# Two head pairs a step, another layout for turned q, and a new order in a sparse-attention and maxout kernel

## The chip, the cores and the metric

One core of one Trainium2 chip. The metric is the device time of one execution in microseconds; times are medians over several runs. Engines in the profile: PE (TensorE matmul) and PEld (its weight loads), DVE (VectorE), ACT (ScalarE), POOL (GpSimd), SP (SyncE, which issues most DMAs here).

## What is computed

Four batches of eight heads, 768 positions, 64 numbers a head. Each query sees the keys less than 16 positions away, and 24 summaries of blocks of 32 positions (the maximum of k, the mean of v, with log 32 added to the score). The result, as 3072 tokens of 512 numbers, goes through a maxout layer. Cut to what matters:

```python
k_sum = k.reshape(B, H, nb, 32, D).max(axis=3)
v_sum = v.reshape(B, H, nb, 32, D).mean(axis=3)
scores_l = where(|i - j| < 16, q @ k.T / sqrt(D), -1e9)
scores_s = q @ k_sum.T / sqrt(D) + log(32)
a = softmax(concat([scores_l, scores_s], axis=-1))
x = (a @ concat([v, v_sum])).transpose(0, 2, 1, 3).reshape(B * S, H * D)
out = maximum(x @ w1, x @ w2) @ w_out
```

## The kernel before, in words

**Work units.** A head pair `hp` is two heads; each batch `b` has four. Each pair's queries fall in three groups `grp` of 256 positions. "Pair 20" means batch 2, pair 0.

**Preparation** (`prep`). k and q are loaded (`load_kq`, L392), cast to bf16 into `kqb`, and turned, so that the 128 numbers of the two heads lie on partitions. For the pairs in `CFG["turn"]` (20 to 23 and 30 to 33, so all of batches 2 and 3) both are turned by a DMA transpose on SP's queue (L519, into `kt`), for the others by PE (L515): k as three f32 transposes of bf16 pairs, q as six bf16 ones. Then `copy` (L483, a helper that records nearly every copy and cast, on whichever engine is chosen) places k in `kx` and q in `qx`. `kx` also takes the wrapped and shared parts and the block maxima `ks` (L541). `qx` holds each head on its own half of the partitions, with zeros in the other half.

**Scores** (`scores`, L599): four matmuls for a group, each 128 keys by 2 x 64 queries, into one PSUM bank. For the pairs in `turn`, q was loaded two tokens a partition, so `qx` has even and odd tokens apart, and the matmul writes every second word:

```python
rhs = qx[b, hp].ap[:].rearrange("p a (m j t) -> p a m j t", m=3, j=2)[:, :, m, :, at:at + half]
to = o[:, :, n0:n1].rearrange("p a (q j) -> p a j q", j=2)
```

In batch 0 the band mask is added on PE (L577, two matmuls with `hide`); in the other batches it is multiplied in on DVE after the exponential (L618, `mask`). The exponential is ACT's (L609), from the bank into `pb`.

**Values** (`values`, L645, L649): eight matmuls (sixteen in batch 0) of `pb` with `vx`, which holds v and the block means; a column of ones gives the sum of the weights. DVE takes its reciprocal (L659, `inv`) and multiplies (L661, into `xs`). Each two pairs are turned to `xt`: in batch 0 by PE (L677), later by a DMA transpose (L668).

**v** (`cast_v`, `spread_v`): v is loaded in pieces of 64 numbers (L401), cast to `vx`, and copied to shifted positions in `vx` ("odd", "all sums": copies of up to 64 x 3168 in batches 1 to 3). Block means are matmuls with `amean` (L451).

**Maxout** (`maxout`, `out_part`): max(a, b) = a + relu(b - a), so the hidden step uses `wd = w2 - w1` (L750, eight matmuls for each of four blocks, then a relu on ACT L759 or DVE L761). `w1o` = w1 x w_out, made once (L734). The output is `xt` x `w1o` (L777, four matmuls) plus `g` x `wo` (L784, eight), copied to `o` and stored.

**The order.** Each step is an `op` of a `Plan` with an estimated time, buffers it reads and writes, and a priority. `CFG["prios"]` gives the priorities and `CFG["engines"]` the engine of each step. `Plan.run` goes through a modelled time, gives every engine the ready step of least priority number, assigns buffer slots from `Ring`s (eight PSUM banks with limits for each kind: `kq` 2, `sc` 2, `av` 2, `mm` 3), and so fixes one instruction order for each engine. On the chip, engines run these fixed lists and wait on semaphores. In the model, DVE and POOL steps on their common port exclude each other.

**Start.** Set-up on POOL builds `hide` (L351 to L364) and `amean` (L370, L373). PE runs 32 matmuls on the identity (`warm_up`, L817) before its first work.

Of the kernel before, what the change touches and what calls it, by code (L numbers as in the profile page):

```python
# [26 lines left out]
    woc=600, wdp=30, lk="ADDP", lq="AAPA", lod="DPS", lse="DDD", lsr="DDS", lvc="DPPPDDAPPAPA", ltl="DDPD", ld=500,  # L27
    turn="20 21 22 23 30 31 32 33", lx="SSS",
)
CFG["prios"] = list(map(int, """  # L30
# [30 lines left out]
""".split()))  # L61
CFG["engines"] = "".join("""
TTPDDDPDAPDDDDDDDPPPDDDPAAPDPPSSSDADATAASSSPPPPTDDSSSPPPPTAASSSPDDPTADSSPPTDSSPPTDSSPATASSDDTDSASDSASDDTATDDADDADTAT
ATAATATDDDDPDATATATAPTATDDPDDDDTATATAATATDDPPPAATATATATDDTDDTATDDTDDTATDDTDDTATDDTDDTATDDTDDTDTDDTDDTDSSSDSSSASSSDSS
SDPDPATDADDTATDDAPADATADTADTADTDDTDDTDDPTATADDPDDATADTADTADTDDSTDDSTDDSPTATADPPAADTADTADTADTDDTDDTDDPTDTADDADAATADTA
DTADTDDSTDDSTDDSSSSPSSSPSSSASSSPPPASTAAPDSDSDDAAPPATADTADTADTDDTDDTDDPSPSDDAPAPATADTADTADTDDSTDDSTDDSDSASDDAADADTADT
ADTADTDDTDDTDDASASDDPPDDATADTADTADTDDSTDDSTDDSSSSPSSSASSSPSSSPPDSATADDPSDSADPPADDTADTADTADTDDTDDTDDDSDSADDADDDTADTAD
TADTDDSTDDSTDDSDSPSDDAPAAPTADTADTADTDDTDDTDDPSASDDAAPDATADTADTADTDDSTDDSTDDSTTATTATTATTATDTDTATDTTTDSTTTASTDTATATATT
TDSTTTDSTDTATATDTTTDSTTTASTATATATATTTDSTTTDSTATATATDTTTASTTTDSTDTATATATTTASTTTASTATATDTATTTDSTTTASTATDTATATTTASTTTAS
TATATATDTTTASTTTASTDTDTATATTTASTTTASTDTDTDTDTTTDSTTTASTATATDTDTTTDSTTTDSTTTAATTTDS  # L70
# [44 lines left out]
class Plan:  # L115
# [3 lines left out]
    BEGIN = {"PE": 1700, "ACT": 1300, "DVE": 850, "POOL": 500, "SP": 0}  # L119
    ISSUE, FIRST, DEPTH = 500, 1100, 5  # L120
# [4 lines left out]
    def op(self, on, us, fn, read=(), write=(), change=(), touch=(), prio=0.0, label="", port=False, issue=None):  # L125

        t = Task()
# [6 lines left out]
        t.fn, t.label, t.may_hold = fn, label, port  # L134
# [23 lines left out]
    def run(self):  # L158
        after = {t: [] for t in self.tasks}
        left = {t: len(t.deps) for t in self.tasks}  # L160
        can = dict.fromkeys(self.tasks, 0)
# [10 lines left out]
        order, events = [], [0, *busy.values()]  # L172
        heapify(events)
        while len(order) < len(self.tasks):
# [4 lines left out]
            for e, queue in open_.items():  # L179
# [7 lines left out]
                if e == "SP":  # L187
                    busy[e] = now + t.issue
                    end = max(sent[-1], now + self.FIRST) + t.us
                    sent.append(end)  # L190
                    t.done = end + max(0, min(1800, 900 + (end - 2300) * 3 // 40 * 10, (16800 - end) * 3 // 200 * 10))
                    heappush(events, busy[e])
                    heappush(events, end)
                else:
                    busy[e] = t.done = now + t.us
                    if t.port:
                        self.held[e] = t.done
# [14 lines left out]
def kernel(  # L212
# [25 lines left out]
    plan = Plan(CFG.get("prios"), CFG.get("engines"))  # L238
    op = plan.op
# [8 lines left out]
    banks = Ring(list(range(8)), {"kq": 2, "sc": 2, "av": 2, "mm": 3})  # L248
# [16 lines left out]
    pbr = Ring(tiles("pb", 10, [128, 4, 192], BF16))  # L265
# [32 lines left out]
    def fixed_parts():  # L298
# [20 lines left out]
        for i, t in enumerate(pbr.slots):  # L319
            once("D", pbr, i, {"D": 0.18, "P": 0.3}, lambda e, t=t: on(e).memset(t[:, :, 64:128], 0.0), i / 3 - 1)  # L320
# [25 lines left out]
        for hs in (slice(0, 4), slice(4, 8)):  # L346
            op("A", {"P": 0.9, "D": 0.85, "A": 1.5}, lambda e, hs=hs: zero(e, by_parity(0)[32:64, 1, :, hs]),
               write=[vx[0], apart_in], prio=0.15, label="gap")
# [5 lines left out]
        def make_hide():  # L354

            nc.gpsimd.memset(hide[:], 0.0)
            by = hide[:].rearrange("p (i w) q -> p w i q", w=2)
            for w, lo, hi, base in ((0, 0, 96, -16), (1, 64, 128, -16), (1, 0, 32, 48)):
                keep(by[lo:hi, w], base + window - 1, 1, [[0, 2], [-1, 64]])
                keep(by[lo:hi, w], window - 1 - base, -1, [[0, 2], [1, 64]])  # L360
            keep(by[96:128, 0], nb - 1, -1, [[0, 2], [0, 64]])
            keep(by[32:64, 1], nb - 1, -1, [[0, 2], [0, 64]])
            nc.gpsimd.memset(hide[64:128, 3, 48:64], NEG)
            nc.gpsimd.memset(hide[0:32, 3, 0:48], NEG)  # L364

        def make_amean():

            for at in (32, 96):
                am = amean[:, :, at:at + nb]
                nc.gpsimd.memset(am, 1.0)  # L370
                for base, mult, pat in ((0, 1, [[128, NM], [-block, nb]]),
                                        (block - 1, -1, [[-128, NM], [block, nb]])):
# [260 lines left out]
    def values(b, hp, grp, pb, prio, xt_on="D"):  # L633
# [20 lines left out]
        if hp % 2 == 0:  # L654
            xs[b, grp] = Buf(xsr)
# [233 lines left out]
```

## Time and profile before

| | us |
|---|---|
| median of 3 runs (range) | 184.57 (184.41 to 184.81) |
| the profiled execution | 183.87 |
| its span in the profile | 182.1 |
| busy: PE / DVE / ACT / POOL | 165.4 / 127.3 / 110.8 / 58.3 |
| instructions: PE / DVE / ACT / POOL | 1658 / 284 / 175 / 89 |

The span is what the profiler saw of the execution; 1.77 us of the execution's time lie outside it. The page gives busy time and 40 slices of the span (each digit is a busy share in tenths). The table of stages gives busy time in chosen stretches. The chain of waits follows the work that ended last back from the end. A matmul's recorded time holds its pipeline latency, so PE's cost of a group is read from the chain, where each piece is the time until the next one: eight hidden matmuls 0.87 us, four of 512 columns 0.86, eight value matmuls 0.24.

### The profile page before, as it was taken

Reading aid. Unit: us, or ns where it says so; the run is one execution under the profiler, and the core shown is the slowest. Engines: PE = TensorE matmul, PEld = TensorE weight load, DVE = VectorE, ACT = ScalarE, POOL = GpSimd, SP = SyncE. Lnnn points to the kernel's source line nnn. Section 1 sums busy time; section 2 is a strip of 40 time slices with the busy share of each in tenths; the row PEclk is TensorE's granted clock in tenths of the full one; section 3 lists DMA queues with packets and bytes.
Section 4 is the critical chain, followed back from the end, with each engine's and each line's share of the span. In section 5 each row is a group of like instructions: output and inputs, shape, how many; then the busy total and the mean of one; then the engine's idle time right before and its main releaser. Section 6 shows DMA issues by size and latency. Waiting matters only on the chain.

```text
span 182.1 us, 4281 instructions
## 1 busy us (share of the span) xinstructions
PE 165.4 (91%) x1658; PEld 119.2 (65%) x1658; DVE 127.3 (70%) x284; ACT 110.8 (61%) x175; POOL 58.3 (32%) x89
## 2 busy tenths in 40 slices
PE   6447998999999995998879999999999999999993
PEld 6335998996664542666557776585757777678453
DVE  6799986769495997999564876684776667334121
ACT  7669895883767779796567566244888453322010
POOL 7867859804050656723510122042121000000000
PEclk9957999999999999999999999999999999999999
DMA  5999999999999964269999799799998035241024
GB/s 180 341 258 271 349 351 363 365 353 219 306 245 218 272 214 124 84 162 229 228 236 238 192 232 283 163 227 239 214 193 229 0 61 144 38 122 48 0 81 155
DMA packets 69589, 37.45 MB, mean 206 GB/s; under 512 B 48640, under 2 KB 65600, under 8 KB 69568
## 3 DMA queue, kind: packets, MB, share of 16 engines
q1 hardware_dynamic: 69424, 37.11, 82.7%
q8 instruction: 13, 0.21, 0.6%
q10 hardware_dynamic: 144, 0.07, 0.1%
q14 instruction: 8, 0.07, 0.1%
HBM read 25.17 MB, written 6.29 MB: 173 GB/s over the span
## 4 chain that ended last, share of the span: by engine, by line
PE 57%; DVE 18%; DMA 12%; ACT 6%; issue 3%; SPq 1%; POOL 1%; POOLq 0%; ACTq 0%; DVEq 0%
PE banks L784 16%; PE banks L750 15%; PE banks L777 8%; PE banks L599 6%; DMA land<-in_v_dram 6%; PE banks L645 5%; DVE pb L618 4%; DMA xt<-xs 3%; DMA land<-in_k_dram 3%; ACT vx L483 3%; DVE kx L483 2%; DVE vx L483 2%; DVE ks L541 2%; PE banks L649 2%; PE banks L515 2%
## 5 line engine op out<-in xcount | busy, mean ns | idle before, releaser
L750 PE MATMUL banks<-xt,wd 128*128 128x256 bf16 x384 | 46.8, 273 | 1.1 <-DMA xt<-xs 1.1
L784 PE MATMUL banks<-wo,g 128*128 128x512 bf16 (+2 forms) x208 | 47.2, 362 | 0.0
L750 PEld LDWEIGHTS <-wd 128*128 128x128 bf16 x384 | 36.7, 98 | 8.2 <-issue 1.2
L609 ACT ACTIVATE pb<-banks 128x512 bf16<-128x512 f32 x48 | 27.0, 595 | 15.1 <-PE banks L599 14.3
L759 ACT ACTIVATE g<-banks 128x512 bf16<-128x512 f32 x29 | 17.2, 597 | 19.2 <-PE banks L750 19.0
L784 PEld LDWEIGHTS <-g 128*128 128x128 bf16 x208 | 18.6, 99 | 15.8
L777 PE MATMUL banks<-w1o,xt 128*128 128x512 bf16 (+2 forms) x104 | 24.7, 363 | 0.0
L645 PEld LDWEIGHTS <-pb 128*128 128x128 bf16 (+1 forms) x384 | 19.2, 98 | 7.5 <-DVE pb L618 3.0
L618 DVE TENSOR_TENSOR pb<-pb,mask 128x512 bf16<-128x512 bf16 (+1 forms) x48 | 21.1, 465 | 4.2 <-ACT pb L609 3.9
L599 PE MATMUL banks<-qx,kx 128*128 128x128 bf16 (+2 forms) x224 | 22.4, 254 | 1.7 <-POOL kx L483 1.5
L645 PE MATMUL banks<-vx,pb 128*128 128x65 bf16 (+1 forms) x384 | 21.1, 193 | 2.2 <-DVE pb L618 1.7
L599 PEld LDWEIGHTS <-kx 128*128 128x128 bf16 x224 | 18.9, 113 | 6.0 <-POOL kx L483 1.7
L761 DVE TENSOR_SCALAR g<-banks 128x512 bf16<-128x512 f32 x19 | 13.1, 691 | 11.8 <-PE banks L750 9.7
L661 DVE TENSOR_TENSOR xs<-banks,inv 128x256 bf16<-128x256 f32 x48 | 19.2, 418 | 0.5
L483 ACT COPY o<-banks 128x512 f32<-128x512 f32 (+1 forms) x14 | 7.9, 565 | 17.1 <-PE banks L784 16.0
L541 DVE TENSOR_REDUCE ks<-kx 128x24 bf16<-128x768 bf16 x16 | 15.1, 945 | 3.3 <-ACT kx L483 3.2
L659 DVE RECIPROCAL inv<-banks 128x4 f32<-128x4 f32 x48 | 7.9, 175 | 12.2 <-PE banks L645 9.5
L483 POOL CAST kqb<-land 128x768 bf16<-128x768 f32 x9 | 9.0, 1010 | 17.8 <-ACT o L483 8.6
L777 PEld LDWEIGHTS <-xt 128*128 128x128 bf16 x104 | 9.6, 100 | 7.3
L483 POOL COPY kx<-kx 128x384 bf16<-128x384 bf16 (+1 forms) x13 | 6.9, 532 | 22.8 <-ACT kx L483 14.0
L483 DVE COPY o<-banks 128x512 f32<-128x512 f32 (+2 forms) x12 | 7.5, 632 | 8.2 <-PE banks L784 8.1
L483 ACT CAST kqb<-land 128x768 bf16<-128x768 f32 x13 | 11.2, 866 | 2.0 <-DMA land<-in_q_dram 1.8
(88 smaller groups left out, 221.1 us busy)
## 6 DMA issues: line engine op xcount, KB each, us to landing
land<-in_k_dram SPq DMA_DIRECT2D x16, 384.0 KB, 5.7
land<-in_q_dram SPq DMA_DIRECT2D x16, 384.0 KB, 5.7
land<-in_v_dram SPq DMA_DIRECT2D x16, 384.0 KB, 6.8
out_dram<-o SPq DMA_DIRECT2D x19, 256.0 KB, 2.5
land<-in_moe_w_dram SPq DMA_DIRECT2D x8, 512.0 KB, 8.6
land<-in_moe_w_out_dram SPq DMA_DIRECT2D x4, 512.0 KB, 9.5
out_dram<-o SPq DMA_DIRECT2D x4, 224.0 KB, 2.7
xt<-xs SPq DMA_TRANSPOSE x18, 3.2
```

The costliest lines, as they stand in the source:

```text
L483: {"D": nc.vector.tensor_copy, "A": nc.scalar.copy, "P": nc.gpsimd.tensor_copy}[e](out=o, in_=i)
L541: op("D", 0.95, lambda e: nc.vector.tensor_reduce(out=ks.ap[:, 0:nb], in_=free(kt(), 128, [256, NM], [192, 2], [32, 2], [1, 32]), axis=AX. ...
L599: nc.tensor.matmul(out=to, lhsT=w, rhs=rhs, start=(mask_on != "T"), stop=(mask_on != "T" or (i == 3 and n1 == 64)))
L609: op("A", 0.61, lambda e: nc.scalar.activation(out=pv(), in_=bank(ps).rearrange("p (i w q) -> p i w q", w=2, q=64), func=ACT.Exp, scale=sc ...
L618: eng.tensor_tensor(out=o, in0=o, in1=m.to_broadcast([128, o.shape[1], 2, 64]), op=ALU.mult)
L645: nc.tensor.matmul(out=av()[:, u, a, :], lhsT=p[r], rhs=vx[b].ap[r, 4 * grp + 2 * u + par, h, 0:D + 1], start=(par == 0), stop=(b > 0 and ...
L661: op("D", 0.42, lambda e: nc.vector.tensor_tensor(out=x.ap[:, hp % 2], in0=av()[:, :, :, 0:D], in1=inv.ap[:].to_broadcast([128, 2, 2, D]), ...
L750: nc.tensor.matmul(out=bank(ps)[:, 256 * s:256 * s + 256], lhsT=wd[n].ap[:, c, 128 * s:128 * s + 128], rhs=x.ap[:, c, :], start=(c == 0), ...
L759: nc.scalar.activation(out=o, in_=bank(ps), func=ACT.Relu)
L761: nc.vector.tensor_scalar_max(out=o, in0=bank(ps), scalar1=0.0)
L777: nc.tensor.matmul(out=bank(ps, c1 - c0), lhsT=x.ap[:, c, sl], rhs=w1o[c].ap[:, cols], start=(c == 0), stop=False)
L784: nc.tensor.matmul(out=bank(ps, c1 - c0), lhsT=g.ap[:, f, sl], rhs=wo[f // 2].ap[:, f % 2, cols], start=False, stop=(f == FC - 1))
```

## The change

- **Two pairs at once.** `scores` now only fills a bank. A new function `weigh` takes the banks of two pairs of one group, with one exponential of 1024 elements into a `pb` of double size, and one mask product (for group 2 four smaller ones). `values` fills two banks, and takes one reciprocal and one product for both. An access pattern steps from one bank to the other. Limits of banks: `sc` 4, `av` 3. `attention` prepares two pairs, then goes through the groups.
- **Turned q.** The pairs in `turn` are now 22, 23, 30 to 33. Their q is loaded with token r of each 128 on partition r, in pieces of 64 numbers, so that `qx` is in plain order after the DMA transpose, and all scores take the plain form.
- **q turned in pairs.** Where PE turns q, it does so as for k: three f32 transposes of bf16 pairs. The cast puts the pairs side by side, and the place reads with a step of two.
- **Set-up.** `hide` is built for 64 columns and copied; `amean` is set with four memsets in place of six instructions on POOL.
- **v copies.** The large "odd" and "all sums" copies of batches 1 to 3 are cut in two halves of the blocks.
- **Order.** New `prios` and `engines`. The plan's model counts PE steps double before 12.5 us and has other start times. No warm-up matmuls (`warm=()`).

The diff, cut to its core:

```diff
-    turn="20 21 22 23 30 31 32 33", lx="SSS",
+    ... relu=1, warm=(), cold=12500,
+    turn="22 23 30 31 32 33", lx="SSS",
...
-    banks = Ring(list(range(8)), {"kq": 2, "sc": 2, "av": 2, "mm": 3})
+    banks = Ring(list(range(8)), {"kq": 2, "sc": 4, "av": 3, "mm": 2 + CFG["relu"]})
-    pbr = Ring(tiles("pb", 10, [128, 4, 192], BF16))
+    pbr = Ring(tiles("pb", 5, [128, 2, 4, 192], BF16))
...
+            nc.gpsimd.memset(hide[:, 0], 0.0)
+            keep(hide[0:96, 0], -16 + window - 1, 1, [[-1, 64]])
+            keep(hide[0:96, 0], window - 1 + 16, -1, [[1, 64]])
+            keep(hide[96:128, 0], nb - 1, -1, [[0, 64]])
...
-                       in_=src[b, 2 * hp:2 * hp + 2].rearrange("h (m p j) d -> p (h m) (j d)", m=3, j=2))
+                       in_=src[b, 2 * hp:2 * hp + 2].rearrange("h (m r) d -> r (h m) d", r=128))
...
+        parts = ((0, NM // 2), (NM // 2, NM)) if whole else ((0, NM),)
...
-                a, to, one = src.ap[:], bank(ps, S, BF16), identity
-                if n == 0:
-                    a, to, one = a.bitcast(F32), bank(ps), ident32
-                for j in range(J if n else J // 2):
+                for j in range(J // 2):
+                    nc.tensor.transpose(out=bank(ps)[:, 128 * j:128 * j + 128],
+                                        in_=src.ap[:].bitcast(F32)[:, 128 * j:128 * j + 128], identity=ident32[:])
...
-                    qx[b, hp].ap[r, a, :], order(qps, [1, 128], [128, J])[r]),
+                    qx[b, hp].ap[r, a, :], order(qps, [2, 128], [256, 3], [1, 2])[r]),
...
-                    if by_dma:
-                        m, at, half = c // 256, c % 256 // 2, (n1 - n0) // 2
...
+                    nc.tensor.matmul(out=view()[:, i // 2, :, i % 2, n0:n1], lhsT=w,
+                                     rhs=qx[b, hp].ap[:, :, c:c + n1 - n0], start=(mask_on != "T"),
...
+    def weigh(b, hp, grp, pss, prio, mask_on):
+        pb, tag = Buf(pbr), f"{b}{hp}{grp}"
+        op("A", {"A": 1.06}, lambda e: nc.scalar.activation(
+            out=spread(pb.ap[:, :, :, 0:128], [4 * 192, 2], [192, 4], [128, 2], [1, 64]),
+            in_=spread(bank_tile[:, pss[0].ap, 0:1], [512 * (pss[1].ap - pss[0].ap), 2], [128, 4], [64, 2], [1, 64]),
+            func=ACT.Exp, scale=scale),
+           read=pss, write=[pb], prio=prio, label=f"exp {tag}")
...
+            if grp < NG - 1:
+                both(spread(pb.ap[:, :, :, 0:128], [192, 8], [128, 2], [1, 64]), 0)
+            else:
+                for i in range(2):
+                    for n in range(2):
+                        both(spread(pb.ap[:, n:n + 1, 2 * i:2 * i + 2, 0:128], [192, 2], [128, 2], [1, 64]), i)
...
+        op("D", 0.19, lambda e: nc.vector.reciprocal(
+            out=inv.ap[:], in_=spread(bank_tile[:, pss[0].ap, D:D + 1], [step(), 2], [D + 1, 4])),
+           read=pss, write=[inv], prio=prio, label=f"inv {tag}")
+        op("D", 0.7, lambda e: nc.vector.tensor_tensor(
+            out=x.ap[:].rearrange("p n u a d -> p n (u a) d"),
+            in0=spread(bank_tile[:, pss[0].ap, 0:1], [step(), 2], [D + 1, 4], [1, D]),
+            in1=spread(inv.ap[:, 0:1, 0:1], [4, 2], [1, 4], [0, D]), op=ALU.mult),
+           read=[*pss, inv], write=[x], prio=prio, label=f"x {tag}")
...
-    for i in range(2):
-        warm_up(i)
     fixed_parts()
+    for n, us, release in CFG["warm"]:
+        warm_up(n, us, release)
```

More of the change, by code (lines that the diff above doesn't have):

```diff
@@ L118, with op @@
     LAG = {"PE": 250, "ACT": 200, "DVE": 150, "POOL": 200, "SP": 800}
-    BEGIN = {"PE": 1700, "ACT": 1300, "DVE": 850, "POOL": 500, "SP": 0}
-    ISSUE, FIRST, DEPTH = 500, 1100, 5
+    BEGIN = {"PE": 1700, "ACT": 2100, "DVE": 1660, "POOL": 310, "SP": 0}
+    ISSUE, FIRST, DEPTH, COLD = 500, 1100, 5, 12500
     def __init__(self, prios=None, engines=None):
         self.tasks, self.prios, self.engines = [], prios, engines
-    def op(self, on, us, fn, read=(), write=(), change=(), touch=(), prio=0.0, label="", port=False, issue=None):
+    def op(self, on, us, fn, read=(), write=(), change=(), touch=(), prio=0.0, label="", port=False, issue=None, release=0):
         t = Task()
@@ L160, in run @@
         left = {t: len(t.deps) for t in self.tasks}
-        can = dict.fromkeys(self.tasks, 0)
+        can = {t: t.release for t in self.tasks}
         for t in self.tasks:
@@ L171, in run @@
         sent = [0] * self.DEPTH
-        order, events = [], [0, *busy.values()]
+        order, events = [], [0, *busy.values(), *can.values()]
         heapify(events)
@@ L194, in run @@
                 else:
-                    busy[e] = t.done = now + t.us
+                    busy[e] = t.done = now + t.us * (2 if e == "PE" and now < self.COLD else 1)
                     if t.port:
@@ L354, in make_hide @@
         def make_hide():
[L356 to L372, printed above, removed]
-                    nc.gpsimd.affine_select(out=am, in_=am, compare_op=ALU.is_ge, fill=0.0, base=base,
-                                            channel_multiplier=mult, pattern=pat)
@@ new lines, in hide_odd, with hide_last, hide_wrap, ones_amean @@
+        def hide_odd(e, lo):
+            on(e).tensor_copy(out=hide[64 - lo:128 - lo, 1], in_=hide[lo:lo + 64, 0])
+        def hide_last(e):
+            on(e).tensor_copy(out=hide[:, 2:4], in_=hide[:, 0:2])
+        def hide_wrap(e):
+            on(e).memset(hide[64:128, 3, 48:64], NEG)
+            on(e).memset(hide[0:32, 3, 0:48], NEG)
+        def ones_amean(e):
+            for j in range(4):
+                on(e).memset(spread(amean[32 * j:32 * j + 32, 0, 32 + j:33 + j], [132, NM], [64, 2]), 1.0)
@@ new lines, in fixed_parts @@
+        half = [Buf(Ring([None])) for _ in range(4)]
+        op("P", 1.0, lambda e: make_hide(), write=[half[0]], prio=-9, label="hide")
+        for n in range(2):
+            op("D", {"D": 0.08, "P": 0.13}, lambda e, n=n: hide_odd(e, 64 * n), read=[half[0]], write=[half[1 + n]],
+               prio=-8, port=True, label="hide odd")
+        op("D", {"D": 0.08, "P": 0.18}, lambda e: hide_last(e), read=half[:3], write=[half[3]], prio=-8, port=True,
+           label="hide last")
+        op("D", {"D": 0.13, "P": 0.2}, lambda e: hide_wrap(e), read=half[3:], write=[hide_in], prio=-8, label="hide wrap")
@@ L379, in fixed_parts @@
+        op("D", {"D": 0.4, "P": 0.7}, lambda e: on(e).memset(amean[:], 0.0), write=[amean_in], prio=-2, label="amean")
+        op("D", {"D": 0.28, "P": 0.45}, lambda e: ones_amean(e), change=[amean_in], prio=0.2, label="amean")
         op("P", 0.4, lambda e: nc.gpsimd.tensor_scalar(
@@ L464, in spread_v, with aps @@
              read=[ps, blocks_in], write=[st], prio=prio, port=False, label=f"sums {tag}")
-        for w, r in ((0, s_rows), (1, slice(32, 64))):
-            def aps(w=w, r=r):
-                ds = slice(0, VW if whole or w == 0 else VW)
-                return (by_parity(b)[r, w, :, hs, ds],
-                        st.ap[r, hs, ds].rearrange("p h d -> p (h d)").rearrange(
-                            "p (o h d) -> p o h d", o=1, d=VW).to_broadcast([32, NM, n, VW]))
-            copy(engines[2], {"D": 0.12 + 6 * n * VW * 0.00028, "P": 0.06 + 6 * n * VW * 0.001,
-                              "A": 0.2 + 6 * n * VW * 0.00083, **({"S": 1.0} if whole else {})}, aps,
-                 read=[st, *([took] if w == 0 else [])], write=out, prio=prio, label=f"all sums {tag}{w}")
+        for i, (w, r, ms) in enumerate((w, r, m) for w, r in ((0, s_rows), (1, slice(32, 64))) for m in parts):
+            cols = (ms[1] - ms[0]) * n * VW
+            def aps(w=w, r=r, ms=ms):
+                return (by_parity(b)[r, w, slice(*ms), hs, :],
+                        st.ap[r, hs, :].rearrange("p h d -> p (h d)").rearrange(
+                            "p (o h d) -> p o h d", o=1, d=VW).to_broadcast([32, ms[1] - ms[0], n, VW]))
+            copy(engines[2], {"D": 0.07 + cols * 0.00029, "P": 0.1 + cols * 0.00086,
+                              "A": 0.2 + cols * 0.00083, "S": 0.5}, aps,
+                 read=[st, *([took] if w == 0 else [])], write=out, prio=prio, label=f"all sums {tag}{i}")
     def copy(engine, us, aps, label, port=True, **kw):
@@ L633, in values, with av, mm @@
     def values(b, hp, grp, pb, prio, xt_on="D"):
-        ps, tag = Buf(banks, "av"), f"{b}{hp}{grp}"
-        def av():
-            return bank(ps)[:, 0:4 * (D + 1)].rearrange("p (u a d) -> p u a d", u=2, a=2)
-        def mm():
+        pss, tag = [Buf(banks, "av") for _ in range(2)], f"{b}{hp}{grp}"
+        def av(n):
+            return bank(pss[n])[:, 0:4 * (D + 1)].rearrange("p (u a d) -> p u a d", u=2, a=2)
+        def mm(n):
             for u in range(2):
@@ L648, in mm @@
                         if b == 0:
-                            nc.tensor.matmul(out=av()[:, u, a, :], lhsT=p, rhs=apart[par][:, h, 0:D + 1],
+                            nc.tensor.matmul(out=av(n)[:, u, a, :], lhsT=p, rhs=apart[par][:, h, 0:D + 1],
                                              start=False, stop=(par == 1))
-        op("T", 0.24 if b else 0.47, lambda e: mm(), read=[pb, ready[b, hp], *([] if b else [apart_of[hp]])], touch=[vx[b]], write=[ps], prio=prio, label=f"values {tag}")
+        for n in range(2):
+            op("T", 0.26 if b else 0.49, lambda e, n=n: mm(n), read=[pb, ready[b, hp + n], *([] if b else [apart_of[hp + n]])],
+               touch=[vx[b]], write=[pss[n]], prio=prio, label=f"values {tag}{n}")
@@ L653, in values @@
         inv = Buf(invr)
-        if hp % 2 == 0:
-            xs[b, grp] = Buf(xsr)
+        x = Buf(xsr)
         if hp == 0:
             xt[b, grp] = Buf(xtr)
-        x, x_t = xs[b, grp], xt[b, grp]
-        op("D", 0.18, lambda e: nc.vector.reciprocal(out=inv.ap[:], in_=av()[:, :, :, D:D + 1]),
-           read=[ps], write=[inv], prio=prio, label=f"inv {tag}")
-        op("D", 0.42, lambda e: nc.vector.tensor_tensor(
-            out=x.ap[:, hp % 2], in0=av()[:, :, :, 0:D],
-            in1=inv.ap[:].to_broadcast([128, 2, 2, D]), op=ALU.mult),
-           read=[ps, inv], write=[x], prio=prio, label=f"x {tag}")
@@ L681, in values @@
         op("T", 0.23, lambda e: turn(), read=[x], write=[xp], prio=prio, label=f"turn x{tag}")
-        copy(xt_on, {"D": 0.42, "A": 0.62}, lambda: (
-            x_t.ap[:, hp - 1:hp + 1, :].rearrange("p h n -> p (h n)"), bank(xp, 512, BF16)), read=[xp], write=[x_t], prio=prio, port=False, label=f"xt {tag}")
-    invr = Ring(tiles("inv", 3, [128, 2, 2, 1], F32))
+        copy(xt_on, {"D": 0.43, "A": 0.6}, lambda: (
+            x_t.ap[:, hp:hp + 2, :].rearrange("p h n -> p (h n)"), bank(xp, 512, BF16)), read=[xp], write=[x_t], prio=prio, port=False, label=f"xt {tag}")
+    invr = Ring(tiles("inv", 3, [128, 2, 4], F32))
     w1t_part = [Buf(Ring([None])) for _ in range(4)]
@@ L743, in maxout, with hid, relu @@
         x, g = xt[b, grp], Buf(gr)
[L744 to L757 removed]
+        per = CFG["relu"]
+        for n0 in range(0, 4, per):
+            pss = [Buf(banks, "mm") for _ in range(per)]
+            for n in range(n0, n0 + per):
+                def hid(n=n, ps=pss[n - n0]):
+                    for s in range(2):
+                        for c in range(KC):
+                            nc.tensor.matmul(out=bank(ps)[:, 256 * s:256 * s + 256],
+                                             lhsT=wd[n].ap[:, c, 128 * s:128 * s + 128],
+                                             rhs=x.ap[:, c, :], start=(c == 0), stop=(c == KC - 1))
+                op("T", 0.87, lambda e, hid=hid: hid(), read=[x, wd[n]], write=[pss[n - n0]], prio=prio, label=f"hidden {b}{grp}{n}")
+            def relu(e, n0=n0, pss=pss):
+                o = spread(g.ap[:, 2 * n0:2 * n0 + 1, 0:1], [512, per], [1, 512])
+                i = spread(bank_tile[:, pss[0].ap, 0:1], [512 * (pss[-1].ap - pss[0].ap) or 512, per], [1, 512])
                 if e == "A":
[L759 removed]
+                    nc.scalar.activation(out=o, in_=i, func=ACT.Relu)
                 else:
[L761 to L763 removed]
+                    nc.vector.tensor_scalar_max(out=o, in0=i, scalar1=0.0)
+            op("A", {"A": 0.17 + 0.43 * per, "D": 0.13 + 0.56 * per}, relu, read=pss, write=[g], prio=-1, label=f"relu {b}{grp}{n0}")
         last = b == B - 1 and grp == NG - 1
```

133 lines of the change are left out of this document (48 added, 85 removed), and 58 rows, old and new, of the table turn.

## The prediction

> **What bounds the kernel now.** I read the page's slices first, then the table of stages, the chain of waits, the groups by form and the timeline where a row was in doubt.
>
> ```profile
> PE   6447998999999995998879999999999999999993
> ...
> PEclk9957999999999999999999999999999999999999
> ```
>
> TensorE has three lives: thin up to about 18 us, full to 50, with gaps to about 93, and then full to 179. The clock falls to half in the third slice although 32 warm-up matmuls ran at the start.
>
> ```profile
> 50.00:60.00 10.00, 9.80 (x72) 5.73 (x71) 7.79 (x13) 7.25 (x12) 2.51 (x3) 1.00 1.25 235
> ...
> 70.00:80.00 10.00, 8.15 (x104) 4.81 (x102) 9.70 (x21) 9.01 (x9) 7.23 (x4) 1.00 0.48 133
> ...
> 110.00:120.00 10.00, 10.00 (x95) 6.27 (x94) 7.64 (x20) 4.95 (x9) 1.09 (x3) 1.00 0.92 239
> ```
>
> Columns: stretch, length, busy time (instructions) of PE, PEld, DVE, ACT, POOL, clock, DMA share, GB/s. Summing what PE lacks: 8.2 us idle in 0 to 20 (its warm-ups count as busy), 0.7 in 20 to 50, 5.0 in 50 to 100, 0.8 at the tail. In 70 to 80 DVE is the full engine; from 100 on PE alone sets the time. So PE work taken from batches 2 and 3 is worth its full length, and work taken from DVE or ACT only before 93 us.
>
> ```profile
> 17.73 0.51 PE banks L515 x6
> ...
> 20.33 0.23 PE banks L599 x5
> ...
> 70.30 2.71 DVE pb L618
> ...
> 99.13 0.44 PE banks L599 x5
> ```
>
> This is the chain: start, length, what. The same five score matmuls of one group take 0.23 us in batch 0 and 0.44 in batch 2, both at clock 1.00. They differ in where they write: heads turned by DMA hold q as even and odd tokens apart, so each matmul writes PSUM in steps of two words. The mask of 2.71 us stands beside a GpSimd copy of 2.83 us (from 69.91); alone it takes 0.41.
>
> **The change part by part.** *q a token a partition, 64 numbers a piece.* Scores of turned heads take the plain form. Batches 2 and 3 have 2 x 4 pairs x 3 groups = 24 groups at 0.44 us, plain ones take 0.22 (four matmuls, chain at 18.45): 24 x 0.22 = 5.3 us less. All lie on PE, and from 92.6 to 160 us the chain itself holds 21 of them (9.24 us). Pairs 20 and 21 leave the turned list, so their k and q cost PE four turns of three f32 transposes, 0.34 us each (chain at 20.90): +1.4. Net on PE **-3.9 us**. SP loses four transposes with 1.2 to 1.3 us of issue each; the 0.35 us DVE places of those q become 0.56 us ones.
>
> The six loads that change are now in 256-byte pieces, as v's are:
>
> ```profile
> 8.00:9.00 1.00, 0.65 (x9) 0.43 (x7) 0.94 (x2) 0.45 (x3) 0.86 (x4) 1.00 1.07 372
> ...
> 10.00:11.00 1.00, 0.45 (x5) 0.18 (x2) 0.97 (x2) 0.00 (x0) 0.81 (x2) 0.50 1.35 229
> ```
>
> The first of these microseconds moves k and q in 1.5 KB pieces, the other v: 372 against 229 GB/s, and 216 in the next one. A load of 393 KB then takes 1.82 instead of 1.06 us at worst, 0.76 more. After 90 us v lands in 5.2 us (median) and q, in 512-byte pieces, in 5.8, so I take 0: PE is full there and works on other groups. Without that cover it costs 6 x 0.76 = 4.6 us. The Trainium skill ("DMA: Bandwidth & Descriptors", Specifications) asks for at least 512 bytes a piece for line rate; the v rows agree, and by it the 4.6 would be paid (a rival below).
>
> *q turned in pairs.* Three f32 transposes take PE as long as six bf16 ones (0.34 each way at full clock), so nothing there. The place on DVE changes form:
>
> ```profile
> L483 DVE COPY qx<-banks 64x768 bf16<-64x768 bf16 x7 | 6.7, 953 | 2.3 <-PE banks L515 2.2
> ...
> L483 DVE COPY kx<-banks 128x768 bf16<-128x768 bf16 x5 | 2.8, 555 | 1.2 <-PE banks L515 1.2
> ```
>
> q should take k's 555 ns: 0.40 less each. Against it the cast of q on ACT or POOL takes k's 1.05 us instead of 0.83, on engines at 61% and 32%: nothing on the path.
>
> *Two head pairs at once.* 48 exps, 48 reciprocals and 48 products become 24 of double size, and the masks of groups 0 and 1 become 12 (group 2 keeps four 256-element ones for two pairs).
>
> ```profile
> 79.26 0.24 DVE L659 RECIPROCAL inv<-banks 128x4 f32<-128x4 f32 x2
> 79.47 0.76 DVE L661 TENSOR_TENSOR xs<-banks,inv 128x256 bf16<-128x256 f32 x2
> ...
> 80.08 1.09 ACT L609 ACTIVATE pb<-banks 128x512 bf16<-128x512 f32 x2
> ```
>
> Two back to back already overlap: two reciprocals 0.24 (one alone 0.175), two products 0.76 (one 0.418), two exps 1.09 (one 0.595). A double product is about 0.69 (512 f32 from PSUM, the relu's row), a double exp about 1.02 (ACT's 1024-element place, 1.014). So a merged pair saves 0.06 to 0.16 on the reciprocal, 0.07 to 0.15 on the product, 0.07 to 0.17 on the exp, about 0.1 on the mask (0.41 for 512, 0.27 for 256, so 0.7 for 1024). DVE: 24 x 0.13 to 0.31 + 12 x 0.1 = 4.3 to 8.6 us; ACT: 1.7 to 4.1. Only the share before 93 us counts. Each merged step makes PE wait for the second half, too: exp +0.43, mask +0.3 before the first product.
>
> *Set-up, warm-ups, order at the start (0 to 20 us).* PE waits for DVE here (busy 14.7 of the first 17.7 us). Before the first reciprocal at 20.19 DVE works 17.1 us; the new list up to that point comes to about 15.4 by the rows (places of q at 0.56, set-up 3.8). GpSimd's mask set-up (1.34 to 4.83 us, and 6.65 to 8.88) shrinks to some seven small instructions, but its first cast at 10.53 waited for the load anyway. I take -1.5. The 32 warm-ups go. They ran 0.112 us apart, half rate by the 0.056 of full clock. A turn of three f32 transposes takes 0.85 us at half clock (at 13.26) and 0.49 at full (59.88): +0.36 for one or two early turns, 0 to +0.7, taken as +0.4, since the clock was at half from 9 to 15 us before, too. A 512 KB weight block goes ahead of the last v (1.5 us at 340 GB/s): 0 while the work of the other three pairs covers it, else +1.5. Sum **-1.1** (ends -2.5 and +1.5). The Trainium skill ("TensorE: Matmul & The Clock Gate", Part 1) has the array start throttled until about 3.4 us of sustained work; by it half of that, 1.7 us, could be lost instead of 0.4, and the sum would be 1.3 higher.
>
> *The middle (50 to 93 us).* DVE is busy 37 of 42.6 us. Nine merged pairs give 1.6 to 3.7 us, two places of q 0.8, and the big v copies are cut in halves, so that the 2.3 us a mask lost beside a GpSimd copy, and the 2 us of a v copy of 3.05 (0.98 alone) at 61 us, can shrink. PE's 5.0 us of gaps cannot shrink by more. The new order decides how much; between -4 and +3 I take **-1.5**.
>
> *The tail.* The last product grows from 0.42 to 0.69, and turning it takes 3.2 us to landing; 0.2 + 0.69 + 3.2 + hand-overs of about 0.4 = 4.5 stand against 4.35 us of PE work queued between (one half of a second product and 32 hidden matmuls): **+0.2**.
>
> **Sum.** -3.9 - 1.1 - 1.5 + 0.2 = -6.3. The profiled execution took 183.87 us (span 182.1 and 1.77 around it), so 177.6; the median of the runs is 0.7 above that execution: **178.3 us**, own range 176 to 181.
>
> **The rivals.** *More: the gaps close.* DVE is relieved enough for PE to run through from 50 us (-4) and to start 2.5 us earlier: 184.6 - 3.9 - 2.5 - 4 + 0.2 = 174.4. For it: DVE is the only full engine in 70 to 80. Against: 10.3 us of the chain from 33 and 5.7 from 45 are loads, which no merge shortens. Chance 0.17.
>
> *The 256-byte loads are paid.* The DMA share is 0.9 to 1.2 in each 10 us from 80 to 140; if the turned q come last, 178.3 + 4.6 = 182.9. Against: PE runs without a gap from 94 us on, so it has other work at hand while a load is late. Chance 0.08, and 0.04 that so much is paid that nothing measurable is left (0.2%, 0.4 us, is about what a measurement of this kernel can tell).
>
> *Slower: pairs stall PE.* Between 50 and 93 us PE has gaps, so a wait is paid in full there: exp +0.43 and mask +0.3 make 0.73 us until the first product of a pair, and two score banks and two product banks are held for it out of eight. Six pairs of batch 1 and two of batch 2 exposed: 8 x 0.73 = 5.8, with nothing gained on the middle or the start: 184.6 - 3.9 + 5.8 + 0.2 = 186.7. It decides from five exposed pairs on (3.9 / 0.73). For it: PE waited 3.0 us for masks in three waits. Against: the second half waited as long before, and the order can put other work between. Chance 0.11.
>
> *It does not do what it says:* the scores' 0.44 would have another cause than the layout; batch 1, loaded plainly, has 0.22 at the same clock, so this only widens the range.
>
> **How the numbers follow.** Forecast 0.60, more 0.17, loads paid 0.08, no change 0.04, slower 0.11. Faster 0.60 + 0.17 + 0.08 = 0.85. The range goes from 174.2 to 184.3, taking in the gap case and the loads case and leaving out the slower one.
>
> **What would show it.** Right: score groups of batches 2 and 3 at 0.22 in the chain, PE's score time down by about 5 us; places of q near 0.56; exps near 1.02; PE idle 50 to 100 of 3 to 4 us; first products of batch 0 at about 17 us. Wrong: score groups still at 0.44; PE waits on masks or exps above 5 us in the middle; PE gaps after 100 us with q loads as releaser.

## The result

The changed kernel takes 193.79 us (median of four runs, 192.87 to 198.05) where the kernel before takes 184.49 beside it: a ratio of 1.0487, 95% interval 1.0429 to 1.0545. It is 9.3 us slower; 178.3 was forecast. Its profiled execution took 192.87 us, with a span of 191.1. Single executions of any of these kernels can be longer than the rest (198.05 us here, 200.54 and 351.52 once each for the kernel before, 606.98 once in e10); the ratios leave such executions out, the medians do not.

The slices of the page, as before:

```profile
PE   0589785999977988899679976999999979998993
...
PEclk9999999999999999999999999999999999999999
```

PE has gaps all along, some of them in the second half, where it ran through before. The same three stages (stretch, length, busy time and instructions of PE, PEld, DVE, ACT, POOL, clock, DMA share, GB/s):

```profile
50.00:60.00 10.00, 7.53 (x55) 4.30 (x53) 7.21 (x17) 7.16 (x10) 2.51 (x5) 1.00 1.08 275
70.00:80.00 10.00, 8.26 (x111) 5.78 (x110) 6.17 (x15) 5.38 (x8) 2.27 (x3) 1.00 0.80 145
110.00:120.00 10.00, 6.74 (x58) 3.85 (x58) 5.04 (x13) 3.40 (x5) 1.23 (x1) 1.00 0.67 167
```

In none of them is any engine full: from 110 to 120 us PE is busy 6.74, DVE 5.04 and ACT 3.40 of 10 us. That is the picture of engines that wait for each other in turn, not of one that became the bound. Idle time of PE by stretch, from the same view of three kernels (e5 is the changed kernel with other bank numbers, see below):

| us | before | changed | e5 |
|---|---|---|---|
| 0 to 20 | 8.2 | 8.4 | 9.3 |
| 20 to 50 | 0.7 | 3.0 | 0.4 |
| 50 to 100 | 5.0 | 7.7 | 0.5 |
| 100 to 150 | 0.0 | 3.7 | 0.0 |
| 150 to the end | 2.8 | 5.0 | 3.5 |

In the first row, the 32 warm-up matmuls of the kernel before (3.6 us) count as busy.

The chain of waits (start, length, what) shows the turns:

```profile
53.66 1.03 ACT pb L603
54.69 0.04 issue
54.73 1.02 PE banks L777 x4
55.76 0.46 PE banks L591 x8
56.22 0.02 issue
56.24 1.03 ACT pb L603
57.27 0.04 issue
57.32 1.04 PE banks L777 x4
58.35 0.02 issue
58.38 1.03 ACT pb L603
59.41 0.04 issue
59.45 1.02 PE banks L784 x4
```

L603 is the double exponential, L777 and L784 are output matmuls of another batch. They have nothing to do with each other: the exp reads score banks and writes `pb`, L777 reads `xt` and `w1o`. Yet each starts when the other has ended. (Four such matmuls cost 0.86 us in a row and 1.02 when they stand alone, so a part of the waiting is booked as busy time.) The view of waits (who waited for whom: total us, times, longest) has the same odd pairs:

```profile
DVE inv L657 <- PE banks L784: 6.6, 3, 3.6
ACT pb L603 <- PE banks L784: 6.5, 1, 6.5
ACT pb L603 <- PE banks L777: 4.4, 4, 1.6
```

The groups (busy us, mean ns of one, then idle time before and its releaser) show that the doubled steps are about as long as they were priced; only the reciprocal is longer, 0.207 us where its savings of 0.06 to 0.16 make 0.18 to 0.19:

```profile
L603 ACT ACTIVATE pb<-banks 128x1024 bf16<-128x1024 f32 x24 | 24.3, 1022 | 26.5 <-PE banks L591 10.0
...
L657 DVE RECIPROCAL inv<-banks 128x8 f32<-128x8 f32 x24 | 5.0, 207 | 22.7 <-PE banks L641 7.3
L660 DVE TENSOR_TENSOR xs<-banks,inv 128x512 bf16<-128x512 f32 x24 | 16.6, 691 | 3.7 <-PE banks L749 2.6
```

### The profile page after: what moved, and what is told of

The parts are those of the page before. It is cut to its first block, busy times and chain, and to the rows that moved or that the text cites. A ratio compares the mean times of both kernels' runs of the same rounds, so it can differ in the third digit from the quotient of the medians.

```text
span 191.1 us, 4050 instructions
## 1 busy us (share of the span) xinstructions
PE 163.3 (85%) x1598; PEld 113.2 (59%) x1598; DVE 117.6 (62%) x236; ACT 104.5 (55%) x143; POOL 57.6 (30%) x86
## 4 chain that ended last, share of the span: by engine, by line
PE 69%; DVE 11%; ACT 9%; DMA 6%; issue 2%; SPq 1%; POOL 1%; DVEq 0%; ACTq 0%; POOLq 0%
PE banks L784 19%; PE banks L749 17%; ACT pb L603 9%; PE banks L777 8%; PE banks L591 6%; PE banks L641 6%; DVE vx L492 4%; DVE xs L660 4%; DMA land<-in_q_dram 4%; PE banks L732 4%; PE banks L520 2%; PE banks L459 2%; DMA xt<-xs 2%; PE banks L581 2%; SPq L399 1%
## 5 line engine op out<-in xcount | busy, mean ns | idle before, releaser
L784 PE MATMUL banks<-wo,g 128*128 128x512 bf16 (+2 forms) x208 | 47.0, 362 | 2.0 <-ACT pb L603 1.1
L603 ACT ACTIVATE pb<-banks 128x1024 bf16<-128x1024 f32 x24 | 24.3, 1022 | 26.5 <-PE banks L591 10.0
L784 PEld LDWEIGHTS <-g 128*128 128x128 bf16 x208 | 18.7, 97 | 19.2 <-issue 2.5
L777 PE MATMUL banks<-w1o,xt 128*128 128x512 bf16 (+2 forms) x104 | 24.2, 362 | 2.5 <-ACT pb L603 1.4
L761 DVE TENSOR_SCALAR g<-banks 128x512 bf16<-128x512 f32 x24 | 16.5, 689 | 15.4 <-PE banks L749 12.5
L591 PE MATMUL banks<-qx,kx 128*128 128x128 bf16 (+2 forms) x208 | 17.5, 219 | 2.6 <-ACT pb L603 1.7
L591 PEld LDWEIGHTS <-kx 128*128 128x128 bf16 x208 | 14.9, 100 | 7.5 <-issue 3.6
L657 DVE RECIPROCAL inv<-banks 128x8 f32<-128x8 f32 x24 | 5.0, 207 | 22.7 <-PE banks L641 7.3
L660 DVE TENSOR_TENSOR xs<-banks,inv 128x512 bf16<-128x512 f32 x24 | 16.6, 691 | 3.7 <-PE banks L749 2.6
L520 PE MATMUL banks<-ident,kqb 128*128 128x128 f32 x60 | 11.9, 323 | 7.8 <-ACT kqb L492 5.4
L611 DVE TENSOR_TENSOR pb<-pb,mask 128x256 bf16<-128x256 bf16 (+1 forms) x36 | 13.9, 428 | 5.6 <-ACT pb L603 5.6
L492 ACT COPY o<-banks 128x512 f32<-128x512 f32 x13 | 7.6, 586 | 17.3 <-PE banks L784 17.3
L777 PEld LDWEIGHTS <-xt 128*128 128x128 bf16 x104 | 9.4, 97 | 11.2 <-issue 1.9
L492 POOL COPY vx<-vx 32x640 bf16<-32x640 bf16 (+5 forms) x12 | 11.7, 973 | 9.7 <-ACT vx L492 8.2
```

The costliest lines, as they stand in the source:

```text
L492: {"D": nc.vector.tensor_copy, "A": nc.scalar.copy, "P": nc.gpsimd.tensor_copy}[e](out=o, in_=i)
L520: nc.tensor.transpose(out=bank(ps)[:, 128 * j:128 * j + 128], in_=src.ap[:].bitcast(F32)[:, 128 * j:128 * j + 128], identity=ident32[:])
L591: nc.tensor.matmul(out=view()[:, i // 2, :, i % 2, n0:n1], lhsT=w, rhs=qx[b, hp].ap[:, :, c:c + n1 - n0], start=(mask_on != "T"), stop=(ma ...
L603: op("A", {"A": 1.06}, lambda e: nc.scalar.activation(out=spread(pb.ap[:, :, :, 0:128], [4 * 192, 2], [192, 4], [128, 2], [1, 64]), in_=sp ...
L660: op("D", 0.7, lambda e: nc.vector.tensor_tensor(out=x.ap[:].rearrange("p n u a d -> p n (u a) d"), in0=spread(bank_tile[:, pss[0].ap, 0:1 ...
L761: nc.vector.tensor_scalar_max(out=o, in0=i, scalar1=0.0)
```

## What was tested

**Theory A.** A double step reads two PSUM banks by one access pattern whose outer step is the distance of the banks (`512 * (pss[1].ap - pss[0].ap)`). The layer that adds the semaphore waits orders such an instruction against work in every bank *between* the two, though it touches none of them. Banks are dealt by the plan as they come free: 15 of the 24 exps have banks that are not neighbours (distances of 2 to 6), and 16 of the 24 reciprocals and products (2 to 7). In the instruction lists of the changed program, 87 of 603 waits between engines join two instructions that share neither a bank nor a buffer (called unneeded below); before it was 9 of 677. The exp at 53.66 in the chain above, on banks 0 and 5, waits for an L777 on bank 1, and the next L777, on bank 2, waits for that exp.

**Theory B.** The slower rival of the prediction: a merged step comes too late for PE, wherever its banks lie, since the first half waits for the second.

**Theory C.** The rival of the loads: q in 256-byte pieces comes too late and starves PE.

Line numbers of the edited kernels are shifted by a few lines.

## The experiments

**Every double step as two one-bank instructions (e1), or only those on distant banks (e2).** Order, engines and banks stay.

```diff
+    def halves(pss, how):
+        near = abs(pss[1].ap - pss[0].ap) == 1
+        return ((0, 1), (1, 1)) if how == "all" or how == "far" and not near else ((0, 2),)
...
+            for n, k in halves(pss, CFG["split_exp"]):    # e1 "all", e2 "far"
+                nc.scalar.activation(
+                    out=spread(pb.ap[:, n:n + 1, :, 0:128], [4 * 192, k], ...),
+                    in_=spread(bank_tile[:, pss[n].ap, 0:1], [512 * (pss[1].ap - pss[0].ap), k], ...
+        # reciprocal and product likewise, by CFG["split_prod"]
```

> The changed kernel with the same order and the same banks, but each exponential, reciprocal and product of a pair written as two instructions of one bank each. Theory A (an instruction that steps from one bank to a far one is ordered against the work in every bank between them, so matmuls and exponentials wait for each other without sharing a bank): these waits go, PE's idle time after 20 us falls from 16 us to 5 to 8, 179 to 184 us. Theory B (the doubled step ends later, so PE waits longer for its data): the masks and the order are as before, so little is won, 190 to 193 us. Theory C (the q loads in 256-byte pieces starve PE): no change, 193 us.

> As the first, but a pair stays one instruction where its two banks are neighbours (9 of 24 exponentials, 8 of 24 reciprocals and products). Theory A: nothing lies between neighbours, so the same time as the first within 1 us. Theory B: a third of the doubled steps is back, so a third of whatever the first won is lost. Theory C: 193 us.

e1: 175.84 us (175.19 to 176.8), ratio to before 0.9531 (0.9491 to 0.957). e2: 175.73 us, 0.9536 (0.9494 to 0.9578). In both, 9 unneeded waits are left. Undoing the merge for the distant pairs alone gives back 18 us, and keeping the near ones merged costs nothing. Both kernels are faster than the changed one and than the kernel before, and e1 is faster than the 179 to 184 us that theory A had expected. Theory C falls here: the loads of q are those of the changed kernel, and the 18 us are gone. The groups of e1 show that the merge hardly shortened the work of DVE:

```profile
L673 DVE TENSOR_TENSOR xs<-banks,inv 128x256 bf16<-128x256 f32 x48 | 18.0, 417 | 0.1
L668 DVE RECIPROCAL inv<-banks 128x4 f32<-128x4 f32 x48 | 6.5, 168 | 11.8 <-PE banks L649 8.7 <-PE banks L653 2.5 <-ACT xt L492 0.3
```

18.0 + 6.5 us of halves against 16.6 + 5.0 of double ones in the changed kernel.

**Only the exps (e3) or only reciprocals and products (e4) split.** `split_exp="all", split_prod="none"`, and the other way round.

> Only the exponentials are split; reciprocals and products stay double. Theory A: 15 of 24 exponentials span far banks and hold PE for up to 1.1 us each, the larger share of the loss, 185 to 189 us. Theory B: exponentials cost 0.43 us of delay a pair, 191 to 193. Theory C: 193.

> Only reciprocals and products are split; exponentials stay double. Theory A: the products' share of the loss goes, 187 to 190 us, and this gain and that of the third run add up to about that of the first. Theory B: 192 to 193. Theory C: 193.

e3: 184.3 us (0.9955, 0.9925 to 0.9986), 54 unneeded waits left. e4: 187.5 us (1.0173, 1.0142 to 1.0204), 51 left. So splitting the exps alone wins 9.5 us (193.8 - 184.3), a little more than expected, splitting the DVE steps alone 6.3 (193.8 - 187.5), and both at once 18.0. The two gains add up to 15.8, not to 18.0; why both together win 2.2 more was not looked into.

**Other bank numbers, nothing else (e5).** All double instructions and the order of every engine stay as in the changed kernel; after planning, each bank gets another number, so that 47 of the 48 pairs lie in neighbours.

```diff
+        for b, slot in zip(HELD, BANKS):   # HELD: the bank buffers in the order made
+            b.slot = int(slot)             # BANKS: one digit for each
         for t in order:
             t.fn(t.letter)
```

> The changed kernel with every double instruction kept and every engine's order kept; only the PSUM bank numbers are dealt out anew, so that the two banks of a pair are neighbours in 47 of 48 cases. Theory A (waits through the banks between): as fast as with split instructions, 175 to 177 us. Theory B (the doubled step itself ends too late): nothing is shortened, 190 to 194 us.

175.89 us (174.39 to 176.49), ratio 0.9519 (0.947 to 0.9568); 7 unneeded waits. Theory B says that merged steps cost time wherever their banks lie; here all are merged and none of the 18 us is paid. B falls, and A is shown by an edit that changes nothing but bank numbers and the waits that follow from them; e2 shows it the other way round, with the banks kept and the distant pairs split. And since e1, with every exp, reciprocal and product split, takes 175.84 us, merging these steps wins nothing that can be measured here. The stages of e5:

```profile
50.00:60.00 10.00, 10.00 (x78) 6.40 (x77) 7.95 (x19) 8.44 (x11) 2.33 (x6) 1.00 1.17 288
70.00:80.00 10.00, 10.00 (x108) 6.66 (x107) 8.51 (x14) 7.09 (x12) 7.36 (x7) 1.00 0.57 117
...
110.00:120.00 10.00, 10.00 (x76) 6.59 (x74) 5.91 (x9) 5.75 (x8) 3.60 (x3) 1.00 1.11 222
```

PE is full in all three. Among the waits of e5, the exps have only their own scores left, and a double exp takes as long as in the changed kernel:

```profile
L611 ACT ACTIVATE pb<-banks 128x1024 bf16<-128x1024 f32 x24 | 24.3, 1026 | 12.5 <-PE banks L599 12.4
...
ACT pb L611 <- PE banks L599: 12.4, 9, 3.4
```

**The mirror: near pairs split, distant ones double (e6).** As e2 with `near` in place of `not near`.

> The mirror image of the second run: pairs in neighbouring banks are split, pairs in far banks stay one instruction. Theory A: all unneeded waits are still there, 192 to 195 us. Theory B: a third of the doubled steps is gone, 186 to 189 us.

196.43 us (1.0616, 1.0559 to 1.0674), with 88 unneeded waits: about as many as in the changed kernel (87), and more instructions. That is the side of theory A, somewhat above its 192 to 195 us.

**One part alone in the old kernel: q a token a partition and plain scores (e7).** The kernel before with only this edit (its turned pairs, order and single steps kept):

```diff
-    in_=src[b, 2 * hp:2 * hp + 2].rearrange("h (m p j) d -> p (h m) (j d)", m=3, j=2))
+    in_=src[b, 2 * hp:2 * hp + 2].rearrange("h (m r) d -> r (h m) d", r=128))
...
-                    if by_dma:
-                        ...
+                    rhs, to = qx[b, hp].ap[:, :, c:c + n1 - n0], o[:, :, n0:n1]
```

> The kernel before with one part of the change: q of the turned pairs loaded a token a partition in 256-byte pieces, and their scores in the plain form; order as before. The prediction's term: 24 groups x 0.22 us = 5.3 us less on PE, 179 to 180 us. If the 256-byte loads are paid: up to 8 x 0.76 = 6 us back, 184 to 186 us.

183.63 us (ten runs), ratio 0.995 (0.9919 to 0.9981): 0.9 us where 5.3 less are spent on scores. The score matmuls did shrink, from 22.4 us (224 of them) to:

```profile
L590 PE MATMUL banks<-qx,kx 128*128 128x128 bf16 (+2 forms) x208 | 17.4, 218 | 3.0 <-POOL kx L483 1.4 <-DVE qx L483 1.3 <-ACT kx L483 0.2
```

but the chain of e7 now has transfers in the part where it had matmuls alone:

```profile
100.20 4.44 DMA kt<-kqb
...
118.57 4.91 DMA kt<-kqb
...
127.47 3.88 DMA land<-in_q_dram
```

PE, which had no gap from 100 to 150 us in the kernel before, is idle there for 2.2 us. The time lies between the two cases expected (179 to 180, and 184 to 186). One reading is that PE works off its queue faster and then waits for k and q of the next pairs, which SP's queue brings in an order made for the slower scores. The other is that the 256-byte loads are paid in part: from 60 to 150 us the packets take 90.7% of the DMA engines' time, 85.3% before, though the seven loads of q issued there land sooner (4.2 us in the median, 4.8 before). e7 changes scores and loads together and does not separate the two; its loads can have cost at most the 4.4 us that are missing of the 5.3.

**The old layout in the new order (e9).** e5 with the two-token loads and the stepped score matmuls put back (the mirror of e7, for the six turned pairs):

> e5_near_banks with one thing put back: q of the six turned pairs (22, 23, 30 to 33) is loaded two tokens a partition in 512-byte pieces as before the change, and their 18 score groups write PSUM in steps of two words again. Order, engines and banks are those of e5 (175.89 us). If the scores' term of the prediction holds in the new order (PE is full from 66 us on), 18 x 0.22 = 4.0 us come back: 179 to 180.5. If the freed PE time is worth as little as in e7_plain_q (0.9 us of 5.3), 176 to 177. If the 256-byte loads of q cost anything in e5, it comes off again here: below 175.5 only if they cost more than the scores gain.

178.11 us (177.08 to 179.1), ratio to before 0.9622 (0.955 to 0.9695). That is 2.2 us above e5 and its repeat e12 (175.89 and 175.91); by the ratios it is 1.9 and 2.8. Its score group:

```profile
L611 PE MATMUL banks<-qx,kx 128*128 128x128 bf16 (+2 forms) x220 | 21.8, 250 | 0.5 <-ACT qx L500 0.5
```

The same group of e5 is 18.0 us, 3.8 less, as 18 x 0.22 = 4.0 says. The answer lies between the two cases expected: about half of the term is left in the new order, under a fifth in the old one (0.9 of 5.3). As in e7, scores and loads change together, so the 256-byte loads of e5 can have cost at most the other 1.8 us.

**No warm-ups in the old kernel (e8).**

> The kernel before without its 32 warm-up matmuls, nothing else changed. The prediction's term: +0 to +0.7 us, taken as +0.4, so 185.0 us. If the array stays at half rate for all of its first work: +1.7 us. If the clock at the start does not matter, since it falls back before the dense work anyway: 184.6.

184.3 us (twelve runs), ratio 0.9998 (0.9974 to 1.0023). Whatever the warm-ups brought in this order is less than about 0.5 us.

**Filler that lasts until the dense work begins (e10, e11; e12 is e5 again).**

```diff
             def turn(src=src, ps=ps):
+                for _ in range(FILL.pop(0) if FILL else 0):     # FILL = [40, 12, 24, 8, 8, 24]
+                    nc.tensor.matmul(out=bank(ps, 128), lhsT=identity[:], rhs=identity[:], start=True, stop=True)
```

> e5_near_banks with filler matmuls on the identity put ahead of the first six PE turns of batch 0 (40, 12, 24, 8, 8, 24 of them, in the gaps before those turns; results overwritten). In e5 PE is dense from 13.8 us but at half rate until about 18 us (a score group 0.43 us, later 0.22). If the half rate there sets the start, fillers that keep PE busy bring the scores to 0.22 from 13.8 us on, and half of 4.1 us is saved: 173.5 to 174.5. If loads, casts and places set the first products anyway, 175.5 to 176.5 although the scores run at 0.22. If the fillers hold up the turns, later than 176.5, with turns that start after their casts by more than 0.3 us.

> The same kernel as e10_near_fill, whose profiled execution was disturbed (606.98 us against 174.26 to 175.47 in the three others), beside e5's kernel in the same call. If the half rate of TensorE before 18 us sets the start, this is 1.5 to 2 us below e12, with score groups at 0.22 us from the first one on. If loads, casts and places set it, it is within 0.7 us of e12 although the scores run at 0.22. If the fillers bring such an execution on, it comes again here.

> The kernel of e5_near_banks again, as the other side of e11: 175.9 us by its earlier runs, first scores at about 14.9 us and at half rate until about 18 us.

e10: 175.31 us, ratio 0.9466 (0.9409 to 0.9523); three of its four executions took 174.26 to 175.47 us. e11: 174.38 us (173.67 to 175.3), ratio 0.9445 (0.9415 to 0.9475). e12: 175.91 us, 0.947 (0.9431 to 0.9509). The timeline of PE in e12 and then in e11 (start, length, what):

```profile
14.88 0.64 PE L599 MATMUL banks<-qx,kx 128*128 128x128 bf16 x5
15.35 0.59 PE L589 MATMUL banks<-hide,identity 128*128 128x256 bf16 x2
15.73 0.63 PE L599 MATMUL banks<-qx,kx 128*128 128x128 bf16 x4
```

```profile
14.65 0.39 PE L602 MATMUL banks<-qx,kx 128*128 128x128 bf16 x5
14.88 0.38 PE L592 MATMUL banks<-hide,identity 128*128 128x256 bf16 x2
15.10 0.39 PE L602 MATMUL banks<-qx,kx 128*128 128x128 bf16 x4
```

With fillers, group follows group every 0.44 us (14.65 to 15.10) instead of every 0.85. The first products start at 18.86 us instead of 20.46 (e12) or 20.23 (e5). How much of that reaches the end is open: the medians differ by 1.5 us, the ratios by 0.0025, which is 0.5 us, and their intervals overlap. So neither expected case is confirmed, neither 1.5 to 2 us nor less than 0.7. No execution of e11 was longer than 175.3 us. Its median is the lowest of this study.

## Why the prediction was wrong, point by point

**The step that failed** is "Two head pairs at once". It priced a merged step by its length, and by "PE wait for the second half, too: exp +0.43, mask +0.3". Its waits were taken for granted: the instruction was treated as if it waited for its own two banks only. It is ordered against every bank from the first to the second, and that cost 18 us (e1, e2, e5). Five of the prediction's six signs of being right came true all the same: score groups at 0.22 us, score time down by 4.9 us (22.4 to 17.5), places of q at 0.553, exps at 1.02, first products at 17.39. Only the sixth, PE's idle time from 50 to 100 us, showed the fault: 7.7 us, not 3 to 4. The diff showed the far step in so many words (`512 * (pss[1].ap - pss[0].ap)`), and the plan's own model of banks knew nothing of it, so the order was made for waits other than those on the chip. "It does not do what it says" was asked of the scores only, not of the waits.

**The slower rival** had the sign (186.7 forecast) but not the mechanism. It had PE wait for a late second half in "six pairs of batch 1 and two of batch 2"; e5 keeps every merged step and has PE idle for 0.5 us from 50 to 100. That rival came closest to the measured time, but not for its reason. The banks that it named as held ("out of eight") were the place, but it counted them and did not ask how far apart they lay.

**The forecast's sum without those waits.** e5 is the changed kernel as it was meant: 175.89 us, 8.7 below the kernel before beside it (184.56), where -6.3 was worked out. So the sign of the sum stands without those waits. That the size is near is partly luck, since the scores brought less than their term and the gaps in the middle closed by more. The terms came out so:

- *Sizes of the merged steps:* exp 1.022 (1.02 forecast), product 0.691 (0.69), mask 0.712 (0.7), place of q 0.553 (0.555), all as read from neighbouring rows. The saving on the reciprocal was mis-sized: 0.207 against 0.24 for two back to back and 0.35 for two alone, so 0.03 to 0.14 and not 0.06 to 0.16. What these savings are worth was overrated: e1 does without those of exp, reciprocal and product and is as fast as e5.
- *Scores, -5.3:* the rate is right. The new layout as a whole is not worth its length, as "So PE work taken from batches 2 and 3 is worth its full length" had it: 0.9 us of 5.3 in the old order (e7), 2.2 of 4.0 in the new one (e9). Where the rest went is open: to a supply that comes no sooner than before, to the smaller pieces of the loads, or to both.
- *256-byte loads at 0:* PE is busy 50.00 of 50 us from 100 to 150 in e5, so their cover held there. The Trainium skill ("DMA: Bandwidth & Descriptors", Specifications) has 512 bytes a piece as the least for line rate; the slower rows of v agree with it, but the 4.6 us that would follow for the turned q were not paid in full in e5: at most 1.8 (e9).
- *The start, -1.1:* first products were to come at about 17 us. Before, they came at 18.51, in the changed kernel at 17.39, in e5 at 20.23. In the last two, a POOL cast of q waits for its load; it starts at 10.88 in the one and 12.70 in the other. What delays that load is open; it goes with the execution and not with the unneeded waits, for e2 has 11.81 and 18.52, and e6, which keeps those waits, 12.57 and 20.32. So the 17.39 was in part luck, and the term is not borne out. *Warm-ups, +0.4:* 0 within about 0.5 us (e8). The Trainium skill ("TensorE: Matmul & The Clock Gate", Part 1) has the array slow until some 3.4 us of sustained work. The traces agree roughly: half rate for 3.2 us of dense work in the kernel before (12.64 to 15.83), 2.8 in the changed kernel (11.97 to 14.80), and at least 4.7 in e12 (13.76 to 18.50; the three f32 transposes at 17.86 still take 0.64 us until the next start, at full rate 0.33). The 1.7 us by the page are not lost by taking the 32 warm-ups away: these ended at 5.4 us, and the dense work of the kernel before started at half rate with them. An estimate from the half rate is that 1.6 of the 3.2 us are lost in the one kernel and 1.4 of the 2.8 in the other; with the fillers of e11 the first products come 1.4 to 1.6 us earlier than in e5 and e12.
- *The middle, -1.5:* mis-sized most. PE's gaps from 50 to 100 us went from 5.0 to 0.5 us in e5, -4.4. "Cannot shrink by more" than 5.0 was right, and nearly all of it went; the rival "the gaps close" (174.4) had this half of it right. The merged exps, reciprocals and products did not do it, since e1, without them, has the same 0.5; the masks, the halved v copies, q turned in pairs, the set-up and the new order were not tested one by one. In the changed kernel the gaps grew to 7.7.
- *The tail, +0.2:* 0.7 us more idle time after 150 us in e5, 2.2 in the changed kernel.

## What to carry over

When an edit joins two operands into one access pattern, ask what range it spans for whoever adds the waits, not what it touches: take neighbouring banks for it, or leave it in two. When no engine is full and the chain alternates between two engines whose steps share no data, look for a wait that should not be there, and compare the waits of the built program with what each instruction reads and writes. Work taken from the full engine can be worth much less than its length (here 0.9 us of 5.3 and 2.2 of 4.0, loads included): ask first whether the others can supply it sooner.

## What the hardware showed besides

A step to a distant bank costs nothing by itself: the double exp takes 1022 ns in the changed kernel and 1026 in e5, where the banks of all 24 exps are neighbours. The Trainium skill ("PSUM — Partial Sum Buffer", PSUM bank collisions raise a hardware error) asks for waits by bank, which for these instructions would be two banks each; the 87 waits beyond that come from the program, not from the chip. No run here leaves out a wait between two instructions on one bank.

The clock row of the page shows full clock over the whole changed kernel and over e12, while their matmuls run at half pace up to 14.8 us in the one and past 18.5 us in the other (three f32 transposes in 0.64 us and later in 0.33); the pace has to be read from the rows.
